# Moving the tail's loads to the sync queue and its stores to the Pool queue in a spectral and gated block with its backward pass

## The chip, the cores and the metric

The kernel runs on one core of a Trainium2 chip. The time is device microseconds of one execution; the time before is the median of three runs. The profile is of one further execution, which took 1523.57 us, and its span is 1521.8 us.

## What is computed

The reference is one block on x of shape 1 x 2048 x 576 in bf16, and the gradients of all its inputs for a given `grad_out`:

```
mod = (silu(c) @ w_mod).reshape(1, 6, 1, 576)       # sa, ca, ga, sb, cb, gb
h = layernorm(x) * (1 + ca) + sa
x = x + ga * irfft2(rfft2(h) * (w_r + 1j * w_i))    # over rows and features
h = layernorm(x) * (1 + cb) + sb
x = x + gb * (((h @ w_gate) * (h @ w_up)) @ w_down) # 4608 inner features
out, vjp = jax.vjp(block, x, w_r, w_i, w_gate, w_up, w_down, c, w_mod)
outputs: out and vjp(grad_out)
```

`out_0` is the block's result, `out_1` the gradient of x, `out_2` and `out_3` those of w_r and w_i (2048 x 289), `out_4` to `out_6` those of w_gate, w_up and w_down, `out_7` that of c, and `out_8` that of w_mod.

## The kernel before

Everything lives in one allocation, `arena`, of 212800 bytes in each of 128 partitions. Views are cut out of it by byte offset (`V`), and a `Ring` hands out a few such views in turn, so a buffer comes free when the last reader of its previous contents is done. The 2048 rows are 16 groups of 128; j is the group.

The order of TensorE's instructions is as the program writes it. The other engines and the DMA queues are ordered by a scheduler, which keeps the data dependencies and the overlaps in `arena`. That order is fixed when the kernel is built: each engine, and each queue of DMA issues, takes its instructions one after the other, and one that waits holds up all behind it. A DMA is issued by SP (`sp`), by ACT (`ac`) or by POOL (`po`). The DMAs of SP and ACT take eight semaphores in turn, so each waits for the one eight places earlier to land.

The stages that come first are forward LayerNorm and spectral filter, and then 18 passes over the gated inner features (gate, up, their gradients). The products `h` of the gated part go to DRAM as `hh_d`. What the change touches is the part after these passes, from about 1190 us on:

- **The LayerNorm rows** (lines 1120 to 1154). For 16 row groups the backward of the second LayerNorm runs (`row_front`, `row_back`), its sums go through TensorE (`row_sums`), and the row group enters the spectral transform (`row_a`). `acc`, a float32 buffer of 16 x 576 in each partition, holds the incoming gradient; rows of it fall free one after the other. The tables of the transform (`TB`, `TC`, `TI`, `TBI`) are loaded into the free rows of `acc`, at j = 14 of this loop as the program is written. `load_wdr` loads `w_down` in three pieces for the output product.
- **The spectral steps** (lines 1265 to 1304, s = 0 to 8). For u = s and u = s - 1: `stage_b`, `turn` (which mirrors half of the weights `Ws[u]`, line 513), `stage_c`, `multiply`, `grad_W` (gradients of w_r and w_i, stored to `out_2` and `out_3`), `store_rev` and `stage_ci`. The weights are loaded by `load_W` (line 508), those of u = 0 and 1 at lines 1232 to 1234.
- **The backward rows of the first LayerNorm** (lines 1336 to 1368, j = 0 to 17). `stage_bi` (lines 569 to 578) and `stage_ai` bring a row group back; `load_xg` loads x (`A_x`) and the gradient `gx1` for it; ScalarE normalises x (line 1349), VectorE and ScalarE do the rest, and the result is stored to `out_1` (line 1355). x, `gx1` and their like are in rings of four. Between them `mod_grad` (lines 1211 to 1217) computes the gradient of w_mod in 18 pieces, with `load_wm2` (line 1209) for its inputs and a store to `out_8`.
- **The output product as filler.** The second half of the forward pass, `hh` times `w_down`, is kept back and cut into 128 pieces of nine matmuls (`y_piece`, line 1074). They stand between the other matmuls, in a queue `fill` that `fill.run(us)` takes pieces from by a credit of 1.1 us each. Four pieces make half a row group in bank 4 or 5, which line 1077 copies out on ScalarE; then line 1081 stores `out_0`. `load_hl` (line 1055) loads 1152 KB of `hh_d` into one of four buffers, and line 1067 the rows of x1.

Of the kernel before, what the change touches and what calls it, by code (L numbers as in the profile page):

```python
# [81 lines left out]
def build(ctx, tc, A_x, A_w_r, A_w_i, B_w_gate, B_w_up, B_w_down, c_in, w_mod, grad_out,  # L82
# [125 lines left out]
    with tc.manual_schedule(engines={PE}):  # L208
# [818 lines left out]
                for i, a in enumerate(srcs):  # L1027
                    mm(bank[w * i:w * i + w, b + h, 0:288], ones[:, 0:w], a[:, 288 * h:288 * h + 288], j == 0, j == 15, skip_group_check=True)

        nx, yl = {}, {}  # L1030

        def acc_h(j):
            return acc[:, j, 288:576].bitcast(BF)
# [18 lines left out]
        def load_hl(k):  # L1052
            jp, half = k // 2, k % 2
            hls[k] = hl_t[k % 4]
            po.dma_start(hls[k][:], hh_d[jp // 2, :, 18 * half:18 * half + 18, 256 * (jp % 2):256 * (jp % 2) + 256])

        yb_r = Ring([ST + 62976, ST + 18688, 1280 + 1152 * SGA], [D])
        xo_r = Ring([ST + 64128, ST + 19840], [D])
# [3 lines left out]
        def y_piece(j, h, i):  # L1062
            def f():
                jp = j // 2
                if h == 0 and i == 0:
                    yst["x"] = xo_r.next()
                    po.dma_start(yst["x"][:], x1_d[:, j, :])
                    yst["y"] = yb_r.next()
                if i == 0:
                    ybank[0] = 9 - ybank[0]  # L1070
                yb = ybank[0]
                for fb in range(9 * i, 9 * i + 9):
                    hl = hls[2 * jp + fb // 18]
                    mm(bank[:, yb, 0:288], hl[:, fb % 18, 128 * (j % 2):128 * (j % 2) + 128], wdr[:, fb, 288 * h:288 * h + 288], fb == 0, fb == 35)  # L1074
                if i == 3:
                    y, x = yst["y"], yst["x"]
                    ac.copy(y[:, 288 * h:288 * h + 288], bank[:, yb, 0:288])  # L1077
                    if h == 1:
                        tt(y[:], y[:], mod[:, SGB, :], MUL)
                        tt(y[:], y[:], x[:], ADD)  # L1080
                        (po if j < 15 else sp).dma_start(o0_v[:, j, :], y[:])
                        if j % 2 == 1:
                            for k in (4 + 2 * jp, 5 + 2 * jp):
                                if k < 16:
                                    load_hl(k)
            return f
# [38 lines left out]
        for j in range(18):  # L1125
            want = min(16, 2 + 5 * j // 4)
            while done < want:
                gh2_last(done)
                done += 1
                if done < want:  # L1130
                    fill.run(1.0)
            while loaded < min(done, j + 3):
                load_n(loaded)
                loaded += 1
            if j < 16:
                row_front(j)
                row_back(j)
            if fill.left() > 12.0 or j > 15:
                fill.run(1.0 if j < 16 else 2.0)
            if 2 <= j < 18:  # L1140
                row_sums(j - 2)
            if fill.left() > 12.0 or j > 15:
                fill.run(1.0)
            if 2 <= j < 18:
                row_a(j - 2)
            if j < 14:
                load1(yl, yl_r, y_d, j + 2, sp)
            if j == 12:
                load_wdr(9, 28)
            if j == 14:  # L1150
                sp.dma_start(TB.rearrange("p a b -> p (a b)"), tabs["TB"][:, :])
                sp.dma_start(TC.rearrange("p a b c -> p (a b c)"), tabs["TC"][:, :])
                sp.dma_start(TI.rearrange("p a b c -> p (a b c)"), tabs["TI"][:, :])
                sp.dma_start(TBI.rearrange("p a b -> p (a b)"), tabs["TBI"][:, :])
        sring = [4, 5]


        RA, RB = ST, ST + 84480
        z_r = Ring(span(RA, 2, U), [4, FP])
        X_r = Ring(span(RA + 2 * U, 2, U) + [ACC + 31168], [2, 2, FP])  # L1160
        W_r = Ring(span(RA + 4 * U, 2, U) + [ACC + 33504], [2, 2, FP])
        P1, P2 = V(RA + 6 * U, [2, 2, FP]), V(RA + 7 * U, [2, 2, FP])
        gw_r = Ring(span(RB, 2, U), [2, 2, FP])
        Q = V(RB + 2 * U, [2, 2, FP], FP32)
        Xl_r = Ring(span(ACC + 24256, 2, U), [2, 2, FP])
        RC = ST + 99200
        ac_r = Ring([RC], [2, FP], FP32)
        Y_t, SD_t = V(RC + U, [2, 2, FP]), V(RC + 2 * U, [4, FP])
# [42 lines left out]
        def mod_grad(s0, rows, k, i):  # L1211
            w, m = wm2[s0, k], 3 * k + i
            ve.scalar_tensor_tensor(out=pr_t[:], in0=w[:, i, :], scalar=1.0, in1=rows, op0=MUL, op1=MUL, accum_out=gsc[:, m, s0 // 2 - 1:s0 // 2])
            ts(w[:, i, :], rows, sc64[:, m:m + 1], None, MUL)
            if i == 2:
                for h in range(2):
                    sp.dma_start(out_8[192 * k:192 * k + 192, (s0 + h) * D:(s0 + h + 1) * D].rearrange("(m q) n -> q m n", q=64), w[64 * h:64 * h + 64])

        mgs = [(2, rows23, k) for k in range(3)] + [(4, rows45, k) for k in range(3)]
        ve.memset(gsc, 0.0)  # L1220
# [4 lines left out]
                for i in range(4):  # L1225
                    yfill.add(1.1, y_piece(j, h, i))

        for t in W_r.t:
            po.memset(t[:, :, :, DF:FP], 0.0)
        Ws, Zs = {}, {}  # L1230
        Xls = {}
        for u in range(2):
            Ws[u] = W_r.next()
            load_W(sp, Ws[u], u)
        load_wdr(28, 36)
        for k in range(2):
            load_hl(k)
# [5 lines left out]
        def grad_W(u, gY):  # L1243
            gw = gw_r.next()
            gt = tt
            gt(Q[:], Xls[u][:], gY[:], MUL)
            gt(gw[:, :, 0, :], Q[:, :, 0, :], Q[:, :, 1, :], ADD)
            gt(Q[:], Xls[u][:], gY[:, :, ::-1, :], MUL)
            gt(gw[:, :, 1, :], Q[:, :, 0, :], Q[:, :, 1, :], SUB)
            for i, o in enumerate((out_2, out_3)):  # L1250
                sp.dma_start(o[u::16, :], gw[:, 0, i, 0:DF])
                if u == 0:
                    sp.dma_start(o[8::16, :], gw[:, 1, i, 0:DF])
            return gw

        def store_rev(u, gw):
            turn(gw, 6)
            for i, o in enumerate((out_2, out_3)):
                sp.dma_start(o[16 - u::16, :], gw[:, 1, i, 0:DF])

        load_X(0)
        load_X(1)
# [2 lines left out]
        for s in range(9):  # L1265
            if 1 <= s < 7:
                Ws[s + 1] = W_r.next()
                load_W(sp, Ws[s + 1], s + 1)
            if s < 8:
                if s == 0:  # L1270
                    fill.run(1.8)
                Zs[s] = stage_b(s, ac_r, z_r)
                fill.run(1.0)
                if s:
                    turn(Ws[s], 6)
                else:
                    spread(rows23, m_sga, m_ssb)
                fill.run(1.2)
                if s == 0:
                    spread(rows45, m_scb, gbh)  # L1280
            if s >= 4:
                store_rev(s - 3, gws[s - 3])
            if s:
                u = s - 1
                Xs[u] = X_r.next()
                stage_c(u, Zs[u], Xs[u], RS)
                multiply(Xs[u], Ws[u], P1, P2, Y_t, SD_t, True, u)
                if u:
                    gws[u - 1] = grad_W(u - 1, Xs[u - 1])
                    if u + 1 < 8:  # L1290
                        load_X(u + 1)
                if s > 1:
                    fill.run(5.0)
                else:
                    fill.flush()
                    fill = yfill
                    for k in range(2, 4):
                        load_hl(k)
                    for t in gw_r.t:
                        po.memset(t[:, :, :, DF:FP], 0.0)  # L1300
                    fill.run(3.0)
                stage_ci(u, Y_t, SD_t, Gt)
                fill.run(1.0 if s < 8 else 2.2)
        gws[7] = grad_W(7, Xs[7])


# [29 lines left out]
        for j in range(18):  # L1336
# [6 lines left out]
            if 1 <= j < 17:  # L1343
                jj = j - 1
                stage_ai(Hs[jj])
                gh = gh_r.next()
                ac.copy(halves(gh), bank[:, 2:4, 0:288])
                n = xl[jj]
                act(n[:], n[:], ACT.Identity, bias=nmr1[:, jj:jj + 1], scale=rstd1[:, jj:jj + 1])
                gn, t2, q, s = tg_r.next(), t2_r.next(), q_r.next(), s_r.next()  # L1350
                gq[jj] = [gh, q]
                ln_bwd_a(gh[:], n, mod[:, SCA, :], gn, q, t2, s)
                ln_bwd_b(n, gn, t2, rstd1[:, jj:jj + 1], gl[jj][:], gn, s)
                o1 = gn
                sp.dma_start(o1_v[:, jj, :], o1[:])
                fill.run(2.2)
            fill.run(2.2)
            if j > 1:
                column_sums(gq.pop(j - 2), 6, j - 2, 64)
            while mdone < min(18, 3 * j // 2):  # L1360
                k, i = mdone // 3, mdone % 3
                mod_grad(*mgs[k], i)
                if i == 2 and k + 2 < 6:
                    load_wm2(mgs[k + 2][0], mgs[k + 2][2])
                mdone += 1
            if 3 <= j < 12:
                i = j - 3
                sp.dma_start_transpose(out=wmT[:, i, :], in_=w_mod[:, 128 * i:128 * i + 128])


# [98 lines left out]
```

## Time and profile before

| | |
|---|---|
| time, median of 3 (lowest to highest) | 1527.02 us (1523.35 to 1529.9) |
| span of the profiled execution | 1521.8 us |
| start of the LayerNorm rows (first store of gx1) | 1195.78 us |
| first spectral matmuls on new weights (line 513) | 1290.92 us |
| first matmul of stage_bi in the backward rows (line 569) | 1391.13 us |
| last matmul (line 1406) ends | about 1517.5 us |
| DMA share of the 16 engines, 1260 to 1340 us | 0.74 |

The page gives for each engine its busy time, and for the whole span a row of tenths. Below that the same is asked for shorter stretches, since the stages of this kernel have different limits. "PE" is the matmul, "PEld" the loading of weights, "DVE" VectorE, "ACT" ScalarE, "SPq" the queue of the sync engine. A wait is written as the waiting instruction, an arrow, and what released it, with the total in us, the number of times and the longest one. The number after L is the line in the kernel before.

### The profile page before, as it was taken

To read this page: it belongs to the slowest core of one execution; us is meant where nothing else is said; L and a number is where in the kernel's file an instruction comes from. 1 tells how busy PE (TensorE), PEld (TensorE's weight loads), DVE (VectorE), ACT (ScalarE), POOL (GpSimd) and SP (SyncE) were. 2 spreads that over 40 slices of the span, in tenths; PEclk is the share of its full clock that TensorE was granted. 3 is DMA by queue.
4 is the path that set the end of the run, shared out by engine and by line. 5 is a ranking of instruction groups with operands and counts; after the bars stand their busy time and mean duration, and the time that the engine had idled before them with its cause. 6 is when DMAs were issued, how large, how long until landed. Compare 5 with 4: busy or idle time off the path is not lost.

```text
span 1521.8 us, 28442 instructions
## 1 busy us (share of the span) xinstructions
PE 1468.4 (96%) x11249; PEld 982.0 (65%) x11272; DVE 780.8 (51%) x1732; ACT 555.2 (36%) x1062; POOL 298.6 (20%) x431
## 2 busy tenths in 40 slices
PE   8999998999999999999999999999999988999788
PEld 5444444667668668668667667767767666776556
DVE  7434596443453353353353354354354874677665
ACT  6766674221221220320321221221221674344455
POOL 1223322202202212211211311311310102111110
PEclk9999999999999999999999999999999999999999
DMA  9655987958557557647646746845854689577862
GB/s 360 155 156 165 227 230 190 201 105 174 132 113 159 138 109 156 150 112 143 161 114 130 164 121 121 172 120 114 182 111 86 179 221 312 146 180 194 254 187 90
DMA packets 406009, 248.65 MB, mean 163 GB/s; under 512 B 318674, under 2 KB 377748, under 8 KB 405364
## 3 DMA queue, kind: packets, MB, share of 16 engines
q1 hardware_dynamic: 376290, 152.98, 46.0%
q0 software_dynamic: 28816, 93.07, 20.4%
q8 instruction: 88, 1.44, 0.4%
q10 hardware_dynamic: 770, 0.80, 0.2%
q14 instruction: 45, 0.37, 0.1%
HBM read 96.46 MB, written 74.20 MB: 112 GB/s over the span
## 4 chain that ended last, share of the span: by engine, by line
PE 80%; DMA 7%; ACT 5%; DVE 4%; issue 3%; POOL 1%; SPq 0%; DVEq 0%; POOLq 0%; ACTq 0%
PE bank L799 9%; PE bank L830 8%; PE bank L801 8%; PE bank L877 8%; PE bank L881 8%; PE bank L1074 5%; PE bank L936 5%; PE bank L939 4%; PE bank L938 4%; PE bank L937 4%; PE bank L367 3%; PE bank L371 3%; PE bank L794 3%; PE bank L897 2%; DMA arena<-in_A_x_dram 2%
## 5 line engine op out<-in xcount | busy, mean ns | idle before, releaser
L950 DVE TENSOR_TENSOR arena<-arena,bank 128x576 f32<-128x576 f32 x256 | 193.0, 754 | 305.1 <-PE bank L939 305.1
L805 ACT CAST arena<-bank 128x512 bf16<-128x512 f32 x144 | 84.4, 586 | 386.5 <-PE bank L795 375.2
L936 PE MATMUL bank<-arena 128*128 128x288 bf16 x576 | 164.0, 285 | 1.5 <-ACT arena L882 1.3
L939 PE MATMUL bank<-arena 128*128 128x288 bf16 x576 | 164.6, 286 | 0.0
L938 PE MATMUL bank<-arena 128*128 128x288 bf16 x576 | 164.3, 285 | 0.0
L937 PE MATMUL bank<-arena 128*128 128x288 bf16 x576 | 164.1, 285 | 0.0
L1074 PE MATMUL bank<-arena 128*128 128x288 bf16 x1152 | 151.5, 288 | 9.1 <-ACT arena L1077 9.1
L881 PE MATMUL bank<-arena 128*128 128x256 bf16 x1152 | 150.2, 274 | 0.0
L877 PE MATMUL bank<-arena 128*128 128x256 bf16 x1152 | 149.5, 273 | 0.6 <-ACT arena L882 0.6
L799 PE MATMUL bank<-arena 128*128 128x512 bf16 x576 | 148.5, 380 | 0.0
L801 PE MATMUL bank<-arena 128*128 128x512 bf16 x576 | 147.8, 379 | 0.0
L1074 PEld LDWEIGHTS <-arena 128*128 128x128 bf16 x1152 | 112.3, 99 | 41.6 <-issue 12.6
L830 PE MATMUL bank<-arena 128*128 128x288 bf16 x1024 | 128.1, 286 | 0.0
L877 PEld LDWEIGHTS <-arena 128*128 128x128 bf16 x1152 | 110.8, 98 | 17.3 <-issue 4.4
L881 PEld LDWEIGHTS <-arena 128*128 128x128 bf16 x1152 | 112.5, 98 | 14.2 <-issue 0.5
L882 ACT CAST arena<-bank 128x256 bf16<-128x256 f32 x144 | 53.5, 371 | 182.2 <-PE bank L881 182.2
L830 PEld LDWEIGHTS <-arena 128*128 128x128 bf16 x1024 | 100.2, 98 | 28.2
L809 DVE TENSOR_TENSOR arena<-arena 128x512 bf16<-128x512 bf16 x144 | 61.2, 425 | 104.3 <-ACT arena L805 102.1
L799 PEld LDWEIGHTS <-arena 128*128 128x128 bf16 x576 | 50.3, 98 | 78.0 <-issue 30.4
L801 PEld LDWEIGHTS <-arena 128*128 128x128 bf16 x576 | 56.4, 98 | 68.0
L727 POOL DMA_DIRECT2D arena<-ghh_d x36 | 20.0, 554 | 394.1 <-DVE arena L808 387.1
L806 ACT CAST arena<-bank 128x512 bf16<-128x512 f32 x144 | 84.8, 589 | 23.1 <-PE bank L801 23.1
(254 smaller groups left out, 2323.1 us busy)
## 6 DMA issues: line engine op xcount, KB each, us to landing
ghh_d<-arena POOLq DMA_DIRECT2D x72, 256.0 KB, 3.8
arena<-ghh_d POOLq DMA_DIRECT2D x36, 512.0 KB, 6.1
hh_d<-arena SPq DMA_DIRECT2D x36, 512.0 KB, 5.4
arena<-hh_d POOLq DMA_DIRECT2D x16, 1152.0 KB, 10.2
out_dram<-arena POOLq DMA_DIRECT2D x36, 256.0 KB, 5.1
out_dram<-arena POOLq DMA_DIRECT2D x51, 144.0 KB, 5.3
arena<-in_B_w_down_dram POOLq DMA_DIRECT2D x18, 288.0 KB, 4.3
arena<-in_B_w_gate_dram POOLq DMA_DIRECT2D x18, 256.0 KB, 3.6
```

The costliest lines, as they stand in the source:

```text
L799: mm(bank[:, bg, :], w[:, m, fs], h2T[:, js, m, :], odd == 0 and m == 0, odd == 1 and m == 3)
L801: mm(bank[:, bu, :], w[:, 4 + k, fs], h2T[:, js, m, :], odd == 0 and k == 0, odd == 1 and k == 3)
L806: ac.copy(u[:], bank[:, bu, :])
L830: mm(bank[:, b0 + h, 0:288], sf[:, 0, fb, j, :], go[:, j, 288 * h:288 * h + 288], j == 0, j == 15)
L877: mm(bank[:, st["b"], 0:256], h2p[:, j, 128 * m:128 * m + 128], sf[:, 1 + w, :, j, :], j == 0, False)
L881: mm(bank[:, st["b"], 0:256], h2p[:, j, 128 * m:128 * m + 128], sf[:, 1 + w, :, j, :], False, j == 15)
L936: mm(o, xT[:, 1, 0, cs], wT[p][:, 0, 0, hs], True, False)
L937: mm(o, xT[:, 2, 0, cs], wT[p][:, 0, 1, hs], False, False)
L938: mm(o, xT[:, 1, 1, cs], wT[p][:, 1, 0, hs], False, False)
L939: mm(o, xT[:, 2, 1, cs], wT[p][:, 1, 1, hs], False, True)
L950: tt(dst, dst, src, ADD)
L1074: mm(bank[:, yb, 0:288], hl[:, fb % 18, 128 * (j % 2):128 * (j % 2) + 128], wdr[:, fb, 288 * h:288 * h + 288], fb == 0, fb == 35)
```

## The change

Five things are changed, all in the last quarter of the span.

1. The loads of `hh_d` and of x1 for the output product go from POOL's queue to SP's. The stores of `out_1`, `out_2`, `out_3` and the pieces of `out_8` from `mod_grad` go from SP's to POOL's. SP then carries the loads of the tail and POOL its stores, so that a load need not stand behind a store which waits for its data.
2. The tables are asked for as soon as rows of `acc` are free (j = 4, 8 and 12 instead of 14), and the weights of the spectral steps 0 and 1 at j = 15 instead of after the loop. For that the ring `W_r` takes the place in `acc` which `Xl_r` had, and `Xl_r` that of `W_r`.
3. After the last spectral step `fill.run` gets 4.4 instead of 2.2, so four pieces of the output product instead of two stand in front of the first `stage_bi`.
4. The pieces of the w_mod gradient are spread over more rows: 6j/5 instead of 3j/2 are done by row j.
5. The transposed loads of w_mod (`wmT`) start at row 5 instead of row 3.

```diff
-        nx, yl = {}, {}
+        nx, yl, Ws = {}, {}, {}
+        W_r = Ring(span(ACC + 24256, 3, U), [2, 2, FP])
...
-            po.dma_start(hls[k][:], hh_d[jp // 2, :, 18 * half:18 * half + 18, 256 * (jp % 2):256 * (jp % 2) + 256])
+            sp.dma_start(hls[k][:], hh_d[jp // 2, :, 18 * half:18 * half + 18, 256 * (jp % 2):256 * (jp % 2) + 256])
...
-                    po.dma_start(yst["x"][:], x1_d[:, j, :])
+                    sp.dma_start(yst["x"][:], x1_d[:, j, :])
...
+            if j == 4:
+                sp.dma_start(TB.rearrange("p a b -> p (a b)"), tabs["TB"][:, :])
+            if j == 8:
+                sp.dma_start(TC.rearrange("p a b c -> p (a b c)"), tabs["TC"][:, :])
             if j == 12:
                 load_wdr(9, 28)
-            if j == 14:
-                sp.dma_start(TB.rearrange("p a b -> p (a b)"), tabs["TB"][:, :])
-                sp.dma_start(TC.rearrange("p a b c -> p (a b c)"), tabs["TC"][:, :])
                 sp.dma_start(TI.rearrange("p a b c -> p (a b c)"), tabs["TI"][:, :])
                 sp.dma_start(TBI.rearrange("p a b -> p (a b)"), tabs["TBI"][:, :])
+            if j == 15:
+                for t in W_r.t:
+                    po.memset(t[:, :, :, DF:FP], 0.0)
+                for u in range(2):
+                    Ws[u] = W_r.next()
+                    load_W(sp, Ws[u], u)
...
-        X_r = Ring(span(RA + 2 * U, 2, U) + [ACC + 31168], [2, 2, FP])
-        W_r = Ring(span(RA + 4 * U, 2, U) + [ACC + 33504], [2, 2, FP])
+        X_r = Ring(span(RA + 2 * U, 2, U) + [ACC + 31264], [2, 2, FP])
...
-        Xl_r = Ring(span(ACC + 24256, 2, U), [2, 2, FP])
+        Xl_r = Ring(span(RA + 4 * U, 2, U), [2, 2, FP])
...
-                    sp.dma_start(out_8[192 * k:192 * k + 192, (s0 + h) * D:(s0 + h + 1) * D].rearrange("(m q) n -> q m n", q=64), w[64 * h:64 * h + 64])
+                    po.dma_start(out_8[192 * k:192 * k + 192, (s0 + h) * D:(s0 + h + 1) * D].rearrange("(m q) n -> q m n", q=64), w[64 * h:64 * h + 64])
...
-                sp.dma_start(o[u::16, :], gw[:, 0, i, 0:DF])
+                po.dma_start(o[u::16, :], gw[:, 0, i, 0:DF])
                 if u == 0:
-                    sp.dma_start(o[8::16, :], gw[:, 1, i, 0:DF])
+                    po.dma_start(o[8::16, :], gw[:, 1, i, 0:DF])
...
-                sp.dma_start(o[16 - u::16, :], gw[:, 1, i, 0:DF])
+                po.dma_start(o[16 - u::16, :], gw[:, 1, i, 0:DF])
...
-                fill.run(1.0 if s < 8 else 2.2)
+                fill.run(1.0 if s < 8 else 4.4)
...
-                sp.dma_start(o1_v[:, jj, :], o1[:])
+                po.dma_start(o1_v[:, jj, :], o1[:])
...
-            while mdone < min(18, 3 * j // 2):
+            while mdone < min(18, 6 * j // 5):
...
-            if 3 <= j < 12:
-                i = j - 3
+            if 5 <= j < 14:
+                i = j - 5
```

## The prediction

> **What bounds the kernel now.** I read the page's busy line first, then the waits of TensorE in the last quarter, then a table of windows for that quarter, then the timeline around the longest gaps.
>
> ```profile
> PE 1468.4 (96%) x11249; PEld 982.0 (65%) x11272; DVE 780.8 (51%) x1732; ACT 555.2 (36%) x1062; POOL 298.6 (20%) x431
> ```
>
> TensorE is busy for 96% of the span and no other engine for more than 51%. The change leaves the number of matmuls alone, so it can only take away idle time of TensorE or slow clock. The first changed instruction is in the LayerNorm rows (from about 1190 us), so only what stands after that counts. Windows of that part (columns: stretch and its length, then busy time and count of PE, PEld, DVE, ACT, POOL, then granted clock, DMA share, GB/s):
>
> ```profile
> 1160.00:1286.00 126.00, 116.85 (x1094) 85.44 (x1091) 90.78 (x242) 73.42 (x155) 18.02 (x27) 1.00 0.72 199
> 1286.00:1391.00 105.00, 95.46 (x771) 70.32 (x772) 68.11 (x105) 39.45 (x90) 15.88 (x22) 0.97 0.73 187
> 1391.00:1492.00 101.00, 87.69 (x672) 59.93 (x672) 66.46 (x186) 56.72 (x123) 15.27 (x20) 0.97 0.69 198
> ```
>
> The spectral steps (1286 to 1391) hold 105.0 - 95.5 = 9.5 us without a matmul, the backward rows of the first LayerNorm (1391 to 1492) 101.0 - 87.7 = 13.3. Who ended it, from the waits of PE between 1150 and 1522 (total us, times, longest):
>
> ```profile
> PE bank L1074 <- ACT arena L1077: 9.1, 3, 4.0
> PE bank L513 <- DMA arena<-in_A_w_r_dram: 5.5, 1, 5.5
> PE bank L571 <- DVE arena L578: 4.0, 4, 2.1
> PE bank L569 <- ACT arena L562: 3.2, 1, 3.2
> ```
>
> Three of these gaps are long, and each stands next to a dip of the clock:
>
> ```profile
> 1290.92 0.81 PE L513 MATMUL bank<-arena 128*128 128x290 bf16 x2 [5.46 <-DMA arena<-in_A_w_r_dram]
> 1391.13 0.55 PE L569 MATMUL bank<-arena 128*128 128x288 bf16 x2 [3.21 <-ACT arena L562]
> 1445.78 2.27 PE L1074 MATMUL bank<-arena 128*128 128x288 bf16 x9 [4.05 <-ACT arena L1077]
> ```
>
> ```profile
> 1289.00:1295.60 6.60, 4.67 (x20) 2.97 (x21) 0.19 (x1) 1.86 (x4) 0.93 (x3) 0.50 0.84 239
> 1391.30:1394.60 3.30, 3.30 (x15) 1.60 (x14) 1.69 (x5) 1.60 (x5) 0.00 (x0) 0.50 0.60 169
> 1446.00:1449.20 3.20, 3.20 (x15) 1.45 (x14) 1.27 (x4) 0.57 (x2) 1.11 (x2) 0.50 1.05 306
> ```
>
> In each of these three windows the granted clock is 0.50. Half of the time that TensorE works there is lost as well: half of 4.67, 3.30 and 3.20 is 2.3, 1.7 and 1.6 us.
>
> The last view is ScalarE in the rows. It stands still for DMA in front of L1349, the normalisation of a row three rows ahead, and what follows it in ScalarE's order (the copies L1077 that free banks 4 and 5, and L575) waits too:
>
> ```profile
> ACT arena L1349 <- DMA arena<-in_A_x_dram: 30.0, 10, 9.1
> ```
>
> **What the Trainium skill says.** "TensorE: Matmul & The Clock Gate", section "What's actually happening": after about 3.4 us without activity the array falls to half clock. The trace agrees: gaps of 5.46, 3.21 and 4.05 us have 0.50 beside them, the 2.86 us gap before 1481.47 has none. "DMA: Bandwidth & Descriptors", section "Queues, rings and completion order": a DMA engine goes round between the queues that have work, and takes descriptors of one ring in order. So a small load issued behind a large one on the same queue starts after it. Before, the large loads of `hh_d` are on POOL's queue and the small ones on SP's, and still the small ones suffer: an x row of 144 KB issued at 1454.28 starts L1349 at 1456.39, 2.1 us later, one issued at 1409.09 behind two `hh_d` loads (1404.78, 1406.63) only at 1418.99, 9.9 us later. "SBUF — State Buffer", section "SBUF: two separate sides": descriptors of POOL's DMAs can be held up while VectorE runs in some modes. No view of this trace separates that.
>
> **The change, part by part.**
>
> *First spectral weights.* Before, the loads of `W` for steps 0 and 1 (L508) are issued from 1277.11 on, together with two `hh_d` loads (POOL, 1274.91 and 1277.07). The real part for step 1, issued at 1279.11, reaches L513 at 1290.9: 11.8 us. After, the static order of SP has these four loads ahead of the last 8-block piece of `wdr` and of the last `gx1` row. SP's loads wait in rotation for the one eight places earlier, here the 2736 KB piece of `wdr` issued at 1251.34 that landed at about 1268.2, the same one that holds the piece at 1268.31 now. So they go out at about 1268.3, 9 us or more earlier, with 22 us to the matmul at 1290.9. Even at 11.8 us they are there by 1281, before TensorE stops at 1285.46. Gap gone: 5.5, half clock gone: 2.3, together 7.8 us. The two `hh_d` loads move behind them on SP at about 1274.7; L1055 takes 7.8/10.2/12.9 us to land (minimum, median, maximum), so the second is there by about 1287.5. The y product starts at about 1287.6 now (1295.4 less 7.8), and reaches the second `hh_d` half two pieces later, at 1289.8. This is tight; I put 0 to 2 us on it, and take 0.
>
> *Tables.* The order of SP has all four in the places they had (the scheduler had moved them up already: TB issued at 1204.29, TC at 1230.40, TI at 1248.60), only TBI comes some entries earlier. Nothing in front of TensorE waits for them: 0.
>
> *More fill work at the last spectral step (2.2 to 4.4).* Two more pieces of the y product (9 matmuls of 0.1225, 1.1 us each by the chain's pieces of 1.10) stand before L569. The wait of 3.21 becomes about 1.0, under the length that cost clock: 2.2 + 1.7 = 3.9 us. Those two pieces are then missing at the end, one between L1374 and L1382, one before L1400. L1400 needs four copies of VectorE (L1387) that the piece hid. A wait of that kind showed 2.3 us as VectorE's wait for L1382 and 0.45 as TensorE's for L1406; I take +1.0, bounds 0.3 and 2.
>
> *Stores to POOL, loads to SP.* SP loses 32 stores of out_2 and out_3, 12 of out_8 and 16 of out_1, and gains 16 `hh_d` and 16 x1 loads. Issue cost is 0.3 to 0.6 us each on both queues, and POOL is 15% busy in the rows: 0. What counts is waiting in order. Before, the x row load of the next rows stood behind stores that waited for VectorE or for other stores (between 1391 and 1492 SP waits 18.7 us in front of L1355 and 5.1 in front of L1209). After, 6 of the 16 x loads (rows 4, 5, 8, 9, 12, 13) stand directly behind one `hh_d` load, which waits for TensorE and then takes perhaps half of the 12 us that a pair takes, some 6 us. Behind the stalled load stand gx1 and the w_mod loads, and for those wait L1349 and L1213. So the x waits do not vanish. But the scheduler has moved ScalarE's order too: in most rows L1077 stands now ahead of L997, and in about half of them L1349 has gone behind L1003. The bank copies are thus freed from a stall in their own row, with 2 us (0.87 + 0.87 + 0.39) more for the load. Of the 9.1 + 1.6 us I take 4 as saved, bounds 10.7 and a loss; the 4.0 of L571 stay.
>
> *w_mod gradients at 6 in 5 rows instead of 3 in 2.* 18 pairs of 0.755 + 0.368 us are 20 us of VectorE over 15 rows instead of 12. VectorE has 66 of 101 us busy: 0, it only smooths. The transposes of `wmT` move two rows: nobody waits for them (needed at L1400): 0.
>
> Sum: -7.8 - 3.9 + 1.0 - 4 = -14.7, so 1527.0 - 14.7 = 1512.3.
>
> **Rivals.** *A, weights only.* The rows gain nothing and the first y piece waits 2 us for `hh_d` on SP's queue, so that 7.8 - 2 + 3.9 - 1 = 8.7 less perhaps 3 us of new waits is left: 1521. For it: the 6 x loads behind `hh_d`. *B, loads on one ring take the place of the stores.* Six x loads land 6 us later, ScalarE has no slack, half of it reaches TensorE (18 us) and three gaps grow past 3.4 us (5 us of clock): 1527 - 11.7 + 1 + 23 = 1539. For it: ScalarE works 56.7 and waits 30.0 of the 101 us. Against it: TensorE lost only 13.3 of those 30, and the two-deep loads fell into the same rows before. *C, all gaps go.* The whole 13.3 + 1.6 us of the rows beside 7.8 and 3.9, less 1.0: 1501.
>
> **How the numbers follow.** Forecast 0.62 (1505 to 1518), A 0.20 (1517 to 1526), B 0.13, C 0.05. Predicted: 1512. The range leaves out B and most of C: 1503 to 1526. 0.5% is 7.6 us, so faster is below 1519.4: 0.62 + 0.05 + a third of A = 0.73; slower above 1534.6: most of B, 0.11; same 0.16.
>
> **What would show it.** L513 no longer waits for `A_w_r`, and no 0.50 clock near 1290. L569's wait is near 1 us. SP's queue has no store in the rows. L1349 still waits for DMA, 20 to 30 us, but L1074 waits less than 6 us for L1077. I am wrong if L1074 waits for `hh_d`, or if VectorE waits for POOL's stores (buffers of `gw`, L1247) so long that L552 on TensorE waits for L525.

## The result, and the profile after

The changed kernel took 1502.76 us (median of 4 runs, 1501.27 to 1503.59) against 1525.78 us for the kernel before on the same chip: a ratio of 0.9845, 95% interval 0.9821 to 0.987. The forecast had the direction, but its gain of 14.7 us was too small: 23.0 us came. 1512.0 us was 9 us too high, and the median lies 0.2 us below the range of 1503 to 1526, with runs on both sides of 1503. The profiled execution has a span of 1501.6 us. Line numbers of the kernel after are one higher than before from L1042 on (L1074 is L1075, L1077 is L1078, L1349 is L1350), and seven higher near L1217; e11 and e14 below are numbered in the same way from L1042 to L1078.

The busy line of the page:

```profile
PE 1469.4 (98%) x11249; PEld 983.5 (66%) x11272; DVE 780.2 (52%) x1732; ACT 555.7 (37%) x1062; POOL 304.2 (20%) x459
```

TensorE works as long as before (1468.4), in a span that is 20.2 us shorter. In this pair of executions all of the difference is idle time of TensorE, and the clock has no part in it: its mean is 0.995 in both. That doesn't hold for the medians, because the profiled execution of the kernel before was a quick one. Its clock is above that of all 89 other executions of that kernel whose clock is on record, 0.985 to 0.994. The 27 beside e2 took 1525.49 to 1536.38 us at 0.985 to 0.992. The four of the kernel after here had 0.995 to 0.998. What the clock is worth is taken up with e3 and e4.

The same table of windows, with the stages where they are now:

```profile
1160.00:1280.00 120.00, 114.44 (x1062) 83.94 (x1061) 91.02 (x242) 70.48 (x150) 13.13 (x21) 0.99 0.71 196
1280.00:1372.00 92.00, 90.90 (x762) 67.58 (x760) 62.92 (x96) 40.69 (x91) 17.04 (x33) 1.00 0.81 208
1372.00:1470.00 98.00, 93.06 (x719) 65.03 (x718) 70.48 (x190) 56.14 (x121) 22.41 (x40) 0.97 0.81 226
```

The spectral steps have 1.1 us without a matmul in place of 9.5, the backward rows 4.9 in place of 13.3. In both the DMA engines are busier (0.81 against 0.73 and 0.69): much the same bytes in less time. The waits of TensorE, from 1150 us to the end (total, times, longest):

```profile
PE bank L571 <- DVE arena L578: 3.6, 3, 1.8
...
PE bank L569 <- ACT arena L575: 0.8, 1, 0.8
```

The three waits that the prediction started from, L1074 for L1077 (9.1), L513 for the weights (5.5) and L569 for L562 (3.2), are all gone in this execution (in after_again L1075 waits 1.9 us for L1078). What is left is the wait of L571, 3.6 now and 4.0 before. ScalarE's wait for x in the rows has got shorter, not gone:

```profile
ACT arena L1350 <- DMA arena<-in_A_x_dram: 21.3, 10, 4.7
```

Its longest stop is 4.7 us and no longer 9.1. Before, stops of 9.10, 6.47 and 5.81 us, each next to a pair of hh_d loads, were followed by waits of L1074 of 2.24, 4.05 and 2.86 us. Now no wait of L1075 follows a stop.

### The profile page after: what moved, and what is told of

Same layout as the page of the kernel before. It is cut to its first block, busy times and chain, and to the rows that moved or that the text cites. A ratio compares the mean times of both kernels' runs of the same rounds, so it can differ in the third digit from the quotient of the medians.

```text
span 1501.6 us, 28451 instructions
## 1 busy us (share of the span) xinstructions
PE 1469.4 (98%) x11249; PEld 983.5 (66%) x11272; DVE 780.2 (52%) x1732; ACT 555.7 (37%) x1062; POOL 304.2 (20%) x459
## 3 DMA queue, kind: packets, MB, share of 16 engines
q0 software_dynamic: 25744, 79.22, 17.3%
## 4 chain that ended last, share of the span: by engine, by line
PE 85%; DVE 5%; ACT 4%; DMA 4%; issue 3%; POOL 0%; SPq 0%; DVEq 0%; ACTq 0%; POOLq 0%
PE bank L799 9%; PE bank L830 8%; PE bank L877 8%; PE bank L801 8%; PE bank L881 8%; PE bank L1075 6%; PE bank L936 5%; PE bank L939 5%; PE bank L938 5%; PE bank L937 5%; PE bank L367 3%; PE bank L371 3%; PE bank L794 3%; PE bank L897 2%; DMA arena<-in_A_x_dram 2%
## 5 line engine op out<-in xcount | busy, mean ns | idle before, releaser
L1075 PE MATMUL bank<-arena 128*128 128x288 bf16 x1152 | 151.9, 290 | 0.0
L1075 PEld LDWEIGHTS <-arena 128*128 128x128 bf16 x1152 | 113.0, 99 | 32.6 <-issue 2.9
L877 PEld LDWEIGHTS <-arena 128*128 128x128 bf16 x1152 | 110.8, 98 | 17.3 <-issue 4.4
```

Source lines behind the costliest of these rows:

```text
L877: mm(bank[:, st["b"], 0:256], h2p[:, j, 128 * m:128 * m + 128], sf[:, 1 + w, :, j, :], j == 0, False)
```

## The experiments

Ratios are to the kernel before on the same chip, with 95% intervals; below 1 is faster. "Idle" is TensorE's idle time from 1150 us on in the profiled run (before: 32.4 us, after: 12.2).

| run | what it is | ratio | idle, us |
|---|---|---|---|
| e2_queues_only | before + the queue swap | 0.9848 (0.9825 to 0.987) | 15.1 |
| e3_loads_only | before + loads of hh_d and x1 on SP | 0.9842 (0.9822 to 0.9862) | 17.3 |
| e13_hh_sp | before + loads of hh_d on SP | 0.984 (0.9823 to 0.9857) | 14.6 |
| e4_stores_only | before + stores on POOL | 1.0011 (1.0001 to 1.0022) | 32.7 |
| e11_before_early_w | before + early spectral weights | 0.9936 (0.9917 to 0.9955) | 27.3 |
| e9_before_fill44 | before + fill 4.4 | 0.9965 (0.9953 to 0.9977) | 29.7 |
| e14_after_old_queues | after, queue swap undone | 0.99 (0.9883 to 0.9917) | 25.5 |
| e1_late_weights | after, weights asked for late | 0.9831 (0.9806 to 0.9855) | 14.8 |
| e5_fill_22 | after, fill 2.2 | 0.9858 (0.9833 to 0.9883) | 17.8 |
| e8_after_x8 | after, eight x buffers | 0.9852 (0.9832 to 0.9873) | 16.9 |
| e15_after_stores_sp | after, stores on SP | 0.9817 (0.98 to 0.9833) | 11.7 |
| after_again | after | 0.9833 (0.9809 to 0.9857) | 16.6 |

### Which edit carries the gain

Theory Q: the queue swap. Its rival: the early weights and the fill, as the prediction's sum has it (P in the expectations, W where it is the weights alone; the P of the later runs on packets is another theory). As recorded, Q also gives a reason, loads that stood behind stores; that part is tested further down. Four runs took the parts apart.

e2_queues_only is the kernel before with `po` and `sp` exchanged as in the diff, and nothing else.

> The kernel before with the queue edits alone: hh_d and x1 loads on SP, stores of out_1, out_2, out_3 and of the out_8 pieces on POOL. Theory Q (the gain of the rows comes from loads that no longer stand behind stores): the waits of TensorE for the copies out of banks 4 and 5 (line 1077) fall from 9.1 us to under 2, time 1510 to 1516 us. Theory P (the gain of the rows comes from the two added filler pieces, which shift where the filler's copies fall in ScalarE's order): these waits stay at 6 us or more, time 1519 to 1528 us.

The whole gain, 0.9848. The wait at L513 is gone though the weights are asked for after the loop as before: SP issues them from 1272.8 to 1276.8 us, and the profile's page for L508 in that stretch says

```profile
DMA to landing us min/median/max: 4.6/4.9/7.0
```

where the kernel before has 11.3/11.7/12.5. The swap carries the gain, by more than Q forecast (1505.64 us against 1510 to 1516), and the rival is wrong.

e9_before_fill44, on the kernel before:

```diff
-                fill.run(1.0 if s < 8 else 2.2)
+                fill.run(1.0 if s < 8 else 4.4)
```

> The kernel before with 4.4 instead of 2.2 at the last spectral step and nothing else. Theory P: the gap in front of stage_bi shrinks (3 to 4 us with its clock) and TensorE's waits for line 1077 fall from 9.1 us to under 2 (with their clock another 8 to 11 us): 1511 to 1515 us. Theory Q: only the first of the two, 1522 to 1523 us, the waits for line 1077 stay.

0.9965, that is 5.4 us (3.5 to 7.2). The wait of L569 for L562 is gone (one of 2.4 us for L575 has come), the others are not:

```profile
PE bank L1074 <- ACT arena L1077: 7.1, 3, 4.9
PE bank L571 <- DVE arena L578: 5.5, 6, 1.6
PE bank L513 <- DMA arena<-in_A_w_r_dram: 4.9, 1, 4.9
```

e5_fill_22 is the same edit the other way round, on the kernel after.

> The changed kernel with 2.2 instead of 4.4 at the last spectral step, so two filler pieces fewer in front of the first backward row. Theory Q: only the gap in front of stage_bi comes back, 2 to 4 us, so 1505 to 1507 us, and the copies out of banks 4 and 5 are still waited for less than 2 us. Theory P: the copies stand at the end of the rows in ScalarE's order again, TensorE waits 5 us or more for them, and the time is 1510 to 1517 us.

0.9858 beside 0.9845 and 0.9833 for the kernel after: 2 to 4 us on the medians, inside the intervals. L569 waits 0.9 us for L562 here, so the wait that the fill was to cover has mostly gone with the queues; its waits for L575 are longer, 5.7 us against 0.8. L1075 waits for no copy, which is against P.

e1_late_weights moves the four loads behind the loop in the program, in the kernel after:

```diff
-                for u in range(2):
-                    Ws[u] = W_r.next()
-                    load_W(sp, Ws[u], u)
...
+        for u in range(2):
+            Ws[u] = W_r.next()
+            load_W(sp, Ws[u], u)
```

> The changed kernel with one part undone: the weights of spectral steps 0 and 1 are loaded after the loop over the LayerNorm rows again, as before (their ring stays in its new place). Theory W (the early load is worth the 5.5 us gap and the half clock behind it): about 7.8 us slower than the changed kernel, so 1510 to 1511 us, and line 513 waits again for the w_r load. Rival (with the queues changed the loads come in time by themselves): 1503 to 1505 us, no such wait.

0.9831: no loss. But the run doesn't test what it was made for. The static order kept the four loads where they had been (issued at 1264.0 to 1266.2 us), so the weights were not late. That late weights are harmless once hh_d is off POOL's queue is shown by e2, not by this run.

### The loads or the stores

> The kernel before, with only the loads of hh_d and x1 moved from POOL's queue to SP's; the stores stay on SP. Theory L (the large hh_d loads on POOL's queue share the 16 DMA engines turn by turn with the small loads of SP, which makes W, x and y take 7 to 12 us; on SP's queue they only stand in line): most of the gain of the queue swap is here, ratio 0.985 to 0.990, no wait of L513 for A_w_r, L1074 waits under 2 us in all for L1077. Theory S (the small loads stood behind stores that waited for their data on SP): little gain or a loss, ratio 0.996 to 1.005, since six x loads now stand behind both stores and hh_d loads; L1074 still waits 6 us or more for L1077.

> The kernel before, with only the stores of out_1, out_2, out_3 and out_8 moved from SP's queue to POOL's; the loads of hh_d and x1 stay on POOL. Theory L: ratio 0.996 or more, L513 still waits 4 to 6 us for A_w_r because hh_d is issued on POOL's queue at the same time, and hh_d loads may now stand behind waiting stores, so that the y pieces wait for them. Theory S: the waits of L1074 for L1077 (9.1 us) and the half clock beside them go, ratio 0.990 to 0.993, while the L513 wait stays, as no store stands in front of those loads.

The loads alone give everything (0.9842), the stores alone nothing (1.0011). With the stores on POOL the old waits stand as they were:

```profile
PE bank L1074 <- ACT arena L1077: 9.5, 3, 4.5
PE bank L513 <- DMA arena<-in_A_w_r_dram: 5.0, 1, 5.0
```

Theory L holds against S, though L1074 still waits 3.2 us for L1077 in e3, where L expected under 2. S, the stated purpose of the swap (a load shouldn't stand behind a store that waits for its data), is wrong for this kernel.

The two runs also show what the clock is worth. Their spans, 1502.9 and 1529.1 us, are 26.2 us apart. TensorE's idle time accounts for 15.4 of that, and for 9.8 its busy time, for the same matmuls (e3, then e4):

```profile
PE 1464.4 (97%) x11249; PEld 980.8 (65%) x11272; DVE 780.5 (52%) x1732; ACT 556.0 (37%) x1062; POOL 270.9 (18%) x399
PE 1474.2 (96%) x11249; PEld 984.4 (64%) x11272; DVE 781.3 (51%) x1732; ACT 555.5 (36%) x1062; POOL 333.0 (22%) x491
```

Between 1150 us and the last matmul, e4 has 23.9 us at half clock (from 1290.1, 1392.5, 1457.3 and 1488.0 us), e3 3.4. Half of the difference is 10.2 us, close to the 9.8.

e13_hh_sp then cuts the edit down to one line:

```diff
-            po.dma_start(hls[k][:], hh_d[jp // 2, :, 18 * half:18 * half + 18, 256 * (jp % 2):256 * (jp % 2) + 256])
+            sp.dma_start(hls[k][:], hh_d[jp // 2, :, 18 * half:18 * half + 18, 256 * (jp % 2):256 * (jp % 2) + 256])
```

> The kernel before with a single line changed: the 16 loads of hh_d (L1055, 1152 KB each) go to SP's queue; x1 stays on POOL, the stores on SP. Theory L (hh_d on POOL's queue is what stretches the small loads): the whole gain of e3_loads_only, ratio 0.982 to 0.988, no wait at L513, under 4 us of L1074 for L1077. Rival X (the x1 loads on POOL, whose packets of 4608 bytes are as large as those of hh_d, stretch them too): ratio 0.989 to 0.994.

0.984, as much as the whole diff, so the x1 loads (rival X) have no part in it. L513 waits no more. In the rows the forecast, under 4 us, was missed:

```profile
PE bank L1074 <- ACT arena L1077: 5.0, 2, 2.7
```

What one line does is best seen around the first weights. The kernel before, POOL's and then SP's issues (start, us, engine, line):

```profile
1274.91 1.25 POOL L1055 DMA_DIRECT2D arena<-hh_d  x1 [0.30 <-DMA arena<-in_B_w_down_dram]
...
1277.07 1.23 POOL L1055 DMA_DIRECT2D arena<-hh_d  x1
```

```profile
1277.11 0.60 SPq L508 DMA_DIRECT2D arena<-in_A_w_r_dram  x1
1277.76 1.25 SPq L508 DMA_DIRECT2D arena<-in_A_w_i_dram  x1
1279.11 1.56 SPq L508 DMA_DIRECT2D arena<-in_A_w_r_dram  x1
```

Two hh_d loads, 2304 KB, are under way when 433 KB of weights are asked for. The hh_d loads land at 1284.7 and 1290.0, the three weights at 1288.4, 1290.3 and 1290.8: large and small end together. With hh_d on SP's queue:

```profile
1273.59 0.44 SPq L1055 DMA_DIRECT2D arena<-hh_d  x1
1274.51 3.14 SPq L508 DMA_DIRECT2D arena<-in_A_w_r_dram  x1
1277.70 0.63 SPq L508 DMA_DIRECT2D arena<-in_A_w_i_dram  x1
1278.44 0.54 SPq L508 DMA_DIRECT2D arena<-in_A_w_r_dram  x1
1279.07 0.42 SPq L508 DMA_DIRECT2D arena<-in_A_w_i_dram  x1
1279.54 0.46 SPq L1055 DMA_DIRECT2D arena<-hh_d  x1
```

One hh_d load is ahead of the weights and the second behind. The weights land at 1281.8 to 1283.2, before TensorE wants them (L513 starts at 1286.19). As far as the trace tells landings, the loads on SP now land in the order in which they were issued. The price shows too: behind hh_d an issue takes 3.14 us, so SP itself is held up, and hh_d lands no earlier (median 10.8 us against 10.2; 7.1 in the kernel after). That is harmless, since the output product asks for it late. Over both later stages a load of weights, x or gx1 that was under way together with an hh_d load took 7.1 us in the median before and 4.9 in e13, of those whose landing the trace tells. This median alone doesn't decide: in the kernel after it is 6.3 us, and 5.6 in after_again.

### The parts together

> The kernel before, with only the early load of the spectral weights of steps 0 and 1 (at row 15 of the LayerNorm loop, in the ring place of the kernel after). The prediction's price for this part is 7.8 us (5.5 of gap and 2.3 of half clock): ratio 0.995. Theory L says that this wait is one of the small loads that the hh_d loads on POOL's queue stretch; an early issue puts W ahead of those hh_d loads, so the wait of L513 goes here as well and the ratio is 0.995 to 0.997, with the waits of L1074 for L1077 left at 7 to 11 us. If the time taken by W is not what L513 waits for but only the first of several, the ratio is 0.999 to 1.001 and a wait of about the same size comes back within 20 us of it.

0.9936, or 9.8 us (6.9 to 12.7), somewhat more than either forecast. The wait at L513 is gone, L1075 waits less than the 7 to 11 us expected, and L571 in the rows waits more:

```profile
PE bank L571 <- DVE arena L578: 8.3, 2, 6.4
PE bank L1075 <- ACT arena L1078: 5.1, 2, 2.9
PE bank L569 <- ACT arena L562: 4.3, 1, 4.3
```

> The kernel after with its queues undone: loads of hh_d and x1 on POOL again, stores on SP again; early W, early tables, fill 4.4 and the new pacing stay. If the early W (0.9936 alone) and the fill (0.9965 alone) add up, ratio 0.989 to 0.991, with L1075 and L571 waiting 8 to 12 us in all for the x loads; the queue edit is then worth some 8 us on top of them and the edits overlap. If they do not add up (the time saved early comes back at a later x load), ratio 0.993 to 0.996. If the queues are needed for all of it, 0.997 or more.

0.99, or 15.3 us (12.7 to 17.9): early weights and fill add up (9.8 + 5.4 = 15.2), and tables and pacing bring nothing that can be seen. The queue edit is worth 8 to 10 us on top of them (0.9845 or 0.9833 less 0.99, of 1530; both together 9.3, give or take 3.7 by the intervals), and 23 us when it stands alone. The two ways overlap by about 15 us: asking early for the weights and moving hh_d cure the same slow load, and the fill covers a wait that hh_d's move removes too.

> The kernel after, with eight x buffers in place of four for the backward rows (in part of acc that is free by then), so that an x row may be loaded seven rows ahead and L1350's 36 us of waiting for DMA falls to under 10. Theory L: nothing in TensorE waits for x any more in the kernel after (its gaps in the rows are 5 us, most of them L571 after L578), so the time stays within 0.3% of the kernel after, ratio to before 0.982 to 0.987. Rival: ScalarE's 36 us of standing still are what sets the pace of VectorE's L578 and so of L571; then another 3 to 6 us go, ratio 0.979 to 0.981.

Eight x buffers change nothing beyond the intervals (0.9852). ScalarE still waits for x, 20.8 us in all where under 10 was expected (the kernel after has 24.8, not the 36 of the expectation), and L571 waits 6.9.

> The kernel after with only its stores back on SP, which might beat both. Moving the stores alone gave 1.0011 on the kernel before, and the loads alone all of the gain, so theory L says that the stores are worth nothing here as well: ratio to before 0.982 to 0.986, within 0.2% of the kernel after. Rival: with loads and stores on one queue the loads stand behind waiting stores, and the stores' move is needed beside that of the loads: ratio 0.987 to 0.991, with L1075 or L571 waiting 3 us more.

0.9817: with its stores back on SP the kernel after loses nothing.

### Why POOL's queue is worse

In the packet records, hh_d on POOL's queue moves in packets of 4096 bytes (207 ns each in the median), on SP's or ScalarE's in 512 (27 ns); x moves in 1152 (51 ns), weights in 578 (31 ns). A packet is here one record of the trace. That suggested theory P of these runs: the engines take a packet from each queue in turn, and large packets starve small ones. e12_hh_act puts the hh_d loads on ScalarE's queue (`ac.dma_start`).

> The kernel before with the 16 loads of hh_d on ScalarE's queue, a second hardware queue beside SP's, instead of POOL's. In the packet records of before, hh_d on POOL's queue moves in packets of 4096 bytes (207 ns each, eight rows of 512 bytes together), the small loads in packets of 1152 bytes (51 ns) or 578 (31 ns); on SP's queue hh_d moves in packets of 512 bytes (27 ns). Theory P (the engine takes a packet from each queue in turn, and 4096 bytes a turn leave the small loads a fifth of the time): on ScalarE's queue the packets are 512 bytes as well, so that small loads land nearly as fast as with hh_d on SP: no wait at L513 over 1 us, ratio 0.984 to 0.992, the rest being ScalarE's own stalls in front of the issues. Rival R (any second queue with a large load hurts, whatever its packets): the L513 wait stays at 3 us or more, L1074 waits 6 us or more for L1077, ratio 0.995 to 1.005. If ScalarE stalls long in front of an issue that waits for a buffer, the ratio may be over 1 under either; then the landing times of W and x in the trace decide (P: under 6 us, R: 8 us or more).

The ratio, 0.9904 (0.9888 to 0.992), lies between POOL and SP and inside P's band. But L513 waits 2.3 us and the first weights take 6.7 to 7.8 us to land, both between the two theories. One long stop remains, and it is an x load again:

```profile
1418.12 0.87 ACT L1349 ACTIVATE arena<-arena 128x576 bf16<-128x576 bf16 x1 [10.68 <-DMA arena<-in_A_x_dram]
```

So packet size and queue had to be separated. With this edit hh_d lies so that one load reads 9216 bytes in a row in each partition:

```diff
-    hh_d = dram("hh_d", [4, 128, 2 * NP, 512])
+    hh_d = dram("hh_d", [8, 128, 2 * NP, 256])
...
-                sp.dma_start(hh_d[:, :, i, :].rearrange("g f x -> f g x"), xT[:, 0, fb, :].rearrange("f (g x) -> f g x", g=4))
+                sp.dma_start(hh_d[:, :, i, :].rearrange("g f x -> f g x"), xT[:, 0, fb, :].rearrange("f (g x) -> f g x", g=8))
...
-            po.dma_start(hls[k][:], hh_d[jp // 2, :, 18 * half:18 * half + 18, 256 * (jp % 2):256 * (jp % 2) + 256])
+            ac.dma_start(hls[k][:], hh_d[jp, :, 18 * half:18 * half + 18, :])
```

(e16 with `ac`, e17 with `sp`, e18 with `po`.)

> As e12_hh_act (kernel before, hh_d loads on ScalarE's queue), but hh_d lies in DRAM so that a load reads 9216 bytes in a row in each partition and not 18 pieces of 512; the stores of hh_d in the 18 passes get rows of 512 in place of 1024 bytes. Theory P (turns by packet, so the size of hh_d's packets decides): the small loads that meet hh_d take 8 us or more in the median (6.4 in e12), L513 waits 4 us or more, ratio 0.996 to 1.010. Theory R (any second queue): as e12, 6 to 7 us, L513 1 to 3 us, ratio 0.988 to 0.993.

> As e13_hh_sp (kernel before, hh_d loads on SP's queue), with hh_d in rows of 9216 bytes as in e16. On one queue the small loads of SP stand in line whatever the packets. Theory P and R both: ratio 0.982 to 0.989, no wait at L513, as e13 (0.984). If the larger packets slow the stores and loads on the other queues so that the time rises to 0.990 or more, or if the rows of 512 bytes in the stores of the passes cost more than 3 us, this run shows it, and e16 must be read against it.

> The kernel before with hh_d in rows of 9216 bytes as in e16 and e17, its loads on POOL's queue as before. Theory T (what counts is how long hh_d holds the engines): if POOL's queue moves the longer rows in larger packets at the 26 bytes a ns that ScalarE's and SP's showed for 9216, in place of the 20 of its 4096 bytes, hh_d lands in 7 to 8 us in place of 10.2, L513 waits 1 to 3 us and the ratio is 0.987 to 0.993. Rival G (POOL's queue as such is bad for the others): the ratio is 0.994 to 1.002, L513 still waits 4 us or more.

| queue of the hh_d loads | pieces of 512 bytes | rows of 9216 bytes |
|---|---|---|
| POOL | 1 (the kernel before) | 0.9931 (0.9908 to 0.9954) |
| ScalarE | 0.9904 (0.9888 to 0.992) | 0.9881 (0.986 to 0.9903) |
| SP | 0.984 (0.9823 to 0.9857) | 0.9806 (0.9788 to 0.9824) |

The packets grew eighteenfold on ScalarE's queue and nothing got worse: 0.9881, and small loads under way beside hh_d took 6.4 and 6.2 us in the median. Theory P, which asked for 8 us and 0.996 or more, has fallen; a smaller effect could hide, since the long rows also shorten hh_d (7.1 us to land in place of 11.3). The stores of the passes don't show: the LayerNorm rows start at 1195.9 to 1197.0 us in e16 to e18. On every queue the ratio is lower with the long rows (on ScalarE's and SP's by 0.0023 and 0.0034, at the edge of what the intervals can tell): 9216 bytes take 347 ns, 26.6 bytes a ns, against 19 to 20 for 512 and 4096. Issue to landing of hh_d on POOL's queue, 10.2 us before, in e18:

```profile
arena<-hh_d POOLq DMA_DIRECT2D x16, 1152.0 KB, 8.1
```

So theory T of the last expectation, that the time for which hh_d holds the engines counts, has some support, though each figure lies just outside its bands: 0.9931, 8.1 us to land, and 3.4 us at L513, between T and G. Small loads beside hh_d took 6.9 us, hardly less than the 7.1 before. But the queue counts at both row lengths, and for more. On its own queue, ScalarE's or POOL's, hh_d isn't held to any place in SP's order.

e20_split_pair asks for the first hh_d load of each pair two pieces of the output product earlier.

> The kernel before with one edit: the first of each pair of hh_d loads is asked for two pieces of the output product earlier (as soon as its buffer is free), so that the two loads on POOL's queue are no longer 2 us apart. Theory T or a theory of bursts: in the rows small loads meet one load of 1152 KB at a time, hh_d lands in 6 to 8 us, L1074 waits under 5 us for L1077; L513 is not touched (the first four loads are as before) and keeps its 5 us: ratio 0.993 to 0.997. Rival G: hh_d lands earlier, but x and gx1 beside it still take 7 us or more, ratio 0.998 to 1.002.

1.0006 (0.9991 to 1.0021), inconclusive: the order of POOL's instructions kept the pairs together (issued at 1406.66 and 1408.52, for one), so the loads were not parted.

### A version that beats both

e19_e15_rows9k is the kernel after with its stores on SP and the long rows.

> e15_after_stores_sp (kernel after with its stores on SP) with hh_d in rows of 9216 bytes, a version that might beat both: fewer packets (18 times fewer for these loads), if a packet of 512 bytes costs more per byte than a large one. In the records 512 bytes take 27 ns and 4096 take 207, so per byte nothing is won: ratio 0.980 to 0.985, within 0.2% of e15 (0.9817).

> The kernel after, on the same chip as e19, so that the move of the stores can be judged side by side: if the stores' move is worth nothing or costs a little, the ratio is 0.982 to 0.985 and that of e19 the same or up to 0.003 lower.

1496.25 us against 1502.64 for the kernel after on the same chip: 0.9791 (0.9769 to 0.9812) beside 0.9833 (0.9809 to 0.9857). It is faster than the kernel after by 6.4 us on the medians; the intervals just touch. e17, the kernel before with the one line and the long rows, is as fast within the intervals: 1498.84 us, 0.9806. TensorE's longest waits from 1150 us on are

```profile
PE bank L439 <- ACT arena L882: 2.5, 2, 2.1
PE bank L571 <- DVE arena L578: 1.9, 3, 0.7
```

L439 belongs to the LayerNorm rows, which the change doesn't speed up. The expectation that long rows bring nothing was probably wrong, as it compared 512 with 4096 bytes only: e16, e17 and e19 are each faster than the run with short rows, by 0.0023 to 0.0034, and e18 by 0.0069.

## Why the prediction was wrong, step by step

- **The bound.** Right. The gain is idle time of TensorE and slow clock.
- **First spectral weights, -7.8.** The size is right: alone it measures 9.8 (6.9 to 12.7), and L513 waits no more. In its arithmetic the loads simply went out earlier. But the wait came from hh_d beside them, and with hh_d on SP the late loads are in time as well.
- **Fill, -3.9, and +1.0 at the end.** Alone 5.4 (3.5 to 7.2) against 2.9: too small, in part because the loss at the end did not come. L1407 waits 0.4 us where L1406 waited 0.45.
- **Queues in the rows, -4 of 10.7. This is the step that failed.** On top of the other edits the queue swap measures 8 to 10 us. Of the 9.1 us of L1074, nothing is left in the profile of after and 1.9 in that of after_again; of the 1.6 there are 0.8 and 1.3 at L569.

What the prediction said of the loads came true. Six x loads stand directly behind one hh_d load on SP, this one among them:

```profile
1424.59 0.41 SPq L1056 DMA_DIRECT2D arena<-hh_d  x1
1429.21 0.33 SPq L1043 DMA_DIRECT2D arena<-in_A_x_dram  x1
```

They take 8.7, 6.4, 6.5 and 3.0 us to land, as far as the trace tells; some 6 was expected. What failed is the price: "So the x waits do not vanish", and with them more than half of TensorE's 10.7 us was to stay. The x waits did stay (21.3 us of 30.0), but in short stops. On SP, hh_d waits only 0.6 us for TensorE in the rows, and its loads come singly, with an x load between them, where POOL's came in pairs 2 us apart. ScalarE's stops at those six x loads are 2.7 us at most; next to the three pairs before they were 9.1, 6.5 and 5.8.

ScalarE's new order, to which the prediction gave part of the saving, can't be ruled out as a helper. In e2 one stop is still 7.2 us long, and no wait of L1074 follows it. There the copy of that row stands ahead of the stop:

```profile
1401.42 0.38 ACT L1077 CAST arena<-bank 128x288 bf16<-128x288 f32 x1
...
1409.32 0.87 ACT L1349 ACTIVATE arena<-arena 128x576 bf16<-128x576 bf16 x1 [7.22 <-DMA arena<-in_A_x_dram]
```

At the three long stops before, L1349 stands ahead of the copy. The scheduler builds the order anew for every edit, so no run parts it from the queue.

- **Half clock, -4.0 of the sum.** Right in kind, but counted on one quick execution. In the profiled pair it happens to cancel: the dips near 1290, 1391 and 1446 are gone, and three others have come, beside short gaps (below). Over the medians it is probably worth more than 4.0 us. e3 and e4 differ by 9.8 us of it. For the kernel after, the mean clocks (0.991 in the seven runs of the kernel before beside after_again, 0.997 in its own four) put it at 9 us at most, an estimate: half clock costs nothing while TensorE is idle.
- **The shortfall.** Of the 8.3 us between 14.7 and 23.0, the rows account for 4 to 6, the fill and the end for 2.5, the weights for 2.0. The clock isn't added to these, because the measured times hold it already.
- **Tables, pacing, wmT at 0.** Nothing contradicts it: early weights and fill account for e14.
- **First y piece, 0 to 2 us for hh_d.** 0 was right; no matmul of L1075 waits for hh_d.
- **Rivals.** C (all gaps go, 1501) was nearest and had 0.05. A (weights only) and B (loads in line take the place of stores) let the x loads behind hh_d cost TensorE as much as the old waits, or more. Those loads took 3.0 to 8.7 us (6.9 to 9.9 beside the pairs before), and no wait of L1075 came of them in the profile of after.
- **What would show it.** Met: L513, no 0.50 near 1290, SP without a store of the rows, L1350 waiting 20 to 30 us for x, L1075 under 6 us. L569 was better than said. VectorE did not come to wait so long for POOL's stores that L552 waits for it: 0.9 us, as before.

Still open: why ScalarE's queue costs less than POOL's (0.9904 against 1), and how the engines share their time between queues. The runs rule out the packet size alone. No run parts two hh_d loads on POOL's queue, so how much of the gain in the rows comes of single loads and how much of the queue isn't known. Nor does a run test the hold-up of POOL's descriptors that the prediction mentioned; POOL's 16 issues of hh_d took 1.2 to 1.4 us each and show no long one.

## What to carry to other kernels

In this kernel a large load that is wanted late was better placed in the queue of the small urgent ones, one at a time among them, than on a queue of its own, where it ran beside them. It is worth trying elsewhere: here it took one line. When a small load takes several times its usual time, look which other transfers are under way at that moment, on whatever queue, before moving the load or adding buffers. And cost edits in company: three edits that measured 9.8, 5.4 and 23 us alone gave 23 to 26 together. And read the granted clock of several executions: the profiled one of the kernel before had a better clock than the 89 others.

## What the hardware showed unexpectedly

The Trainium skill, "DMA: Bandwidth & Descriptors", section "Issuing engines are not separate DMA queues", has transfers of all issuing engines interleave on the same engines. The runs agree, and show what it costs: for one set of loads the choice between three queues was worth 24 us.

Long rows: in the records of the traces 9216 bytes in a row moved at 26.6 bytes a ns, the 4096 of POOL's queue (eight rows of 512) at 19.8, single rows of 512 at 19.0.

The clock. Three windows of the kernel after, at half clock with TensorE busy nearly throughout:

```profile
1242.80:1246.20 3.40, 3.25 (x15) 1.88 (x13) 2.56 (x9) 3.40 (x9) 0.77 (x1) 0.50 1.05 215
1413.50:1416.80 3.30, 3.30 (x16) 2.07 (x15) 2.99 (x9) 3.00 (x8) 0.00 (x0) 0.50 0.78 204
1440.80:1444.10 3.30, 3.30 (x15) 2.10 (x14) 3.30 (x11) 2.32 (x7) 0.66 (x1) 0.50 0.21 63
```

The gap ahead of the first was 1.95 us (L439). Those ahead of the last two are short as well:

```profile
1411.28 0.41 PE L569 MATMUL bank<-arena 128*128 128x288 bf16 x2 [0.80 <-ACT arena L575]
1412.72 0.41 PE L571 MATMUL bank<-arena 128*128 128x288 bf16 x2 [1.03 <-DVE arena L578]
```

```profile
1440.11 0.41 PE L571 MATMUL bank<-arena 128*128 128x288 bf16 x2 [1.75 <-DVE arena L578]
```

So the clock fell after gaps of 0.80 and 1.03 us close together, and after ones of 1.75 and 1.95, where the prediction had put the threshold near 3.4 us; its own gap of 3.21 was shorter already. That these gaps were the cause isn't shown. In after_again a gap of 2.11 us before the same L571 had no dip beside it, and its span is 1501.7 us, with 4.4 us more idle time. So with equal spans one execution lost time to gaps, the other to half clock (mean 0.998 and 0.995). In all 20 profiled executions a stretch at half clock lasts 3.4 us or a multiple of it (6.8, 10.2, and 13.7 in e12), but for the last one of each, which the end cuts off.
